# A linear-attention and MLP kernel: inverting the chunk triangles through the lower half's rows in 128 partitions, with one joining product instead of two

## The chip, the cores and the metric

The kernel runs on one core of one Trainium2 chip. The metric is the device time of the program in microseconds; three runs of the kernel before gave 593.81, 594.18 and 589.45 us, a median of 593.81. The profile is that of one further execution, of 596.33 us.

## The reference

A state matrix of 40 x 40 for each of 4 batches and 8 heads (32 in all) goes through 768 steps; its rows are read out before each step. What comes out is normalised and goes through an MLP with a residual.

```python
def _attn_ref(r, k, v, w, a, b):
    state = np.zeros((B, H, D, D))
    for t in range(S):
        y[:, :, t] = einsum('bhd,bhde->bhe', rt, state)
        Sa = einsum('bhde,bhe->bhd', state, at)
        state = state * wt[:, :, None, :] - einsum('bhd,bhe->bhde', Sa, bt) \
                + einsum('bhd,bhe->bhde', vt, kt)

def _moe_ref(x, g_ln, w_ch1, w_ch2):
    xn = (x - mean) / sqrt(var + 1e-06) * g_ln      # x: [4, 768, 320]
    return x + maximum(xn @ w_ch1, 0) @ w_ch2       # 320 -> 1280 -> 320
```

All inputs are float32: B, H, S, D = 4, 8, 768, 40.

## The kernel before

The 768 steps are cut into 24 chunks of C = 32 steps. Inside a chunk the dependence of a step on the earlier ones is a strictly lower triangular 32 x 32 matrix for each of the 32 heads (batch and head together), and the kernel needs the inverse of one plus that triangle. So a chunk has these parts:

- `prep` (L324): two scans on DVE (L338, L342) make running products of the decays; POOL multiplies them into the inputs (L350, L356; for chunks 0 and 1 DVE does it); PE forms all products of a chunk's steps with each other (L366); DVE gives them their sign and moves them out of PSUM (L369). One half of the result goes to DRAM as the triangles, `d_l`.
- `invert` (L396) makes the inverses. It works on a slab: chunks 0 and 1 are slabs of one chunk, done on DVE; all later slabs are two chunks, done on POOL. A triangle is one partition, so a slab of two chunks has 64 partitions of 32 x 32 elements.
- `merge` (L427) loads the inverted halves into `hv` in the layout that PE wants, and PE completes the inverse, `tt`.
- `chain` (L487): PE reads out the state with the chunk's rows (L498), ACT copies it (L501), PE multiplies by `tt` (L508), ACT copies that (L512), PE forms the state's update (L523) and DVE adds it (L532, L533). This is what one chunk must have of the one before.
- `post` (L540) makes the chunk's output rows from these (L551, L563, L578, L595).
- `norm` and `moe` normalise each chunk's 128 rows and run the MLP for two chunks at a time, in ten pairs of groups of dense matmuls: eight of L766 and six of L750 each. ACT (L769) and DVE (L771) stand between them.

The inverse in the kernel before is made of 16 x 16 halves (B = 16). A triangle [[P, 0], [Q, R]] has the inverse [[P', 0], [-R'QP', R']], with a prime for an inverse (the sign is in the data). `invert` inverts P and R at the same time, side by side in the free dimension of the same partition: for j from 1 to 14 a multiplication (L416) of column j by row j into `ytmp` and an addition (L420) into the rows below, over [64, 2, 15-j, j] elements. Before them stands a memset of the diagonal (L408), after them a copy on ACT that transposes R' (L422). A DMA stores P' and R' in `d_h`, and another copies Q from `d_l` to `d_h` inside DRAM (L425). `merge` then has two products: L441 forms QP' (16 columns) with an identity carried in the same operand, ACT copies it into `qm` (L443), and L452 forms the rest (32 columns), which ACT copies into `tt` (L454). Both have 32 matmuls, 8 heads in each of 4 quadrants of the array. The trace has two records for each.

What sets the order: `Plan` (L50) is given each operation with its engine, its assumed time in us, its due time (a key in chunks) and what it reads and writes. It goes through them as a list scheduler on an assumed clock and writes out one fixed order for each engine; the engines then work in that order and wait for each other by semaphores. An operation that is late on one engine so holds back all that stands behind the waiting one. Operations with `lock=True` on DVE and POOL are kept apart in the plan. DMAs are all issued from SP, in order, and take turns on eight semaphores, so that a DMA also waits for the one that was eight before it. In the plan a pair of L416 and L420 costs 0.54 us on DVE and 0.9 on POOL.

Of the kernel before, what the change touches and what calls it, by code (L numbers as in the profile page):

```python
# [11 lines left out]
F32 = mybir.dt.float32  # L12
# [4 lines left out]
ALU = mybir.AluOpType  # L17
# [4 lines left out]
C = 32  # L22
B = C // 2
# [159 lines left out]
def body(ctx, tc, ea, eb, vr, rd, vt, w1, w1x_in, w2, gl, fe, fd, out):  # L183
# [64 lines left out]
    d_h = [dr.tile([32 * n, B, 3 * B], F32, name=f"d_h{s}") for s, (_, n) in enumerate(SLABS)]  # L248
# [15 lines left out]
    def consts():  # L264
# [16 lines left out]
        for i in range(2):  # L281

            op("DVE", 0.9, -99 + i, (), [("wa", i, 0)], lambda i=i: V.memset(wa[i][32:64], 1.0))
        for i in range(BK):
            op("POOL", 0.9, -99 + i, (), [("bk", i, 0)], lambda i=i: G.memset(bk[i][32:64], 1.0))
        op("POOL", 0.3, -84, (), ["qm"], lambda: G.memset(qm, 0.0))
# [11 lines left out]
        for i in range(2):  # L298
# [3 lines left out]
            def f(i=i):  # L302
                for q, qs in enumerate(QUADS):
                    up, lo = (ident[qs, 32 * q + B * x:32 * q + B * x + B].unsqueeze(1).broadcast_to([32, 8, B])
                              for x in range(2))
                    A.copy(out=hv[i][qs, :, 0:B], in_=lo)
                    A.copy(out=hv[i][qs, :, 4 * B:5 * B], in_=up)
                    if i == 0:
                        A.copy(out=qm[qs, :, 0:B], in_=lo)
            op("ACT", 2.6 if i == 0 else 1.8, -50 + i, ["ident"], two("hv", i, 4) + (["qm"] if i == 0 else []), f)  # L310
# [85 lines left out]
    def invert(s):  # L396

        c0, n = SLABS[s]
        p0 = 32 * (c0 % 2)
        L = [("d_l", s, x) for x in range(2 * n)]  # L400
        Y = [("y", c0 % 2)] if n == 1 else [("y", 0), ("y", 1)]
        n *= 32
        eng, e, us = ("DVE", nc.vector, 0.54) if c0 < 2 else ("POOL", nc.gpsimd, 0.9)
        k0 = c0 - 2.0 - 2 * soon(c0)
        y = yv[p0:p0 + n]
        rows = y[:, 0:1024].rearrange("p (a t) -> p a t", t=C)
        dma(k0, 262, L, Y, y[:, 0:1024], d_l[s].rearrange("m a t -> m (a t)"))
        op(eng, 0.15, k0, (), Y, lambda: e.memset(y[:, 0:1024:33], 1.0))  # L408
        yb = y.rearrange("p (i x) -> p i x", i=2)[:, :, 0:512].rearrange("p i (a t) -> p i a t", t=C)[:, :, :, 0:B]
        for j in range(1, B - 1):  # L410
            m = B - 1 - j
            S = [n, 2, m, j]

            def f(j=j, m=m, S=S):
                tv = tmp[p0:p0 + n, 0:2 * m * j].rearrange("p (i a t) -> p i a t", i=2, t=j)
                e.tensor_tensor(  # L416
                    out=tv, in0=yb[:, :, j + 1:, j:j + 1].broadcast_to(S),
# [551 lines left out]
```

## Time and profile before

| what | value |
|---|---|
| runs, median (lowest to highest) | 593.81 us (589.45 to 594.18) |
| the profiled execution, its time | 596.33 us |
| its span in the profile | 594.6 us |
| mean granted clock of TensorE | 0.961 |
| PE busy | 517.6 us, 87% |
| DVE busy | 410.9 us, 69% |
| ACT busy | 311.2 us, 52% |
| POOL busy | 276.2 us, 46% |
| bytes moved by DMA | 58.58 MB in 119670 packets |

In the profile PE is the matmul stream of TensorE and PEld its loading of weights, which runs beside it; DVE is VectorE, ACT ScalarE, POOL GpSimd; SPq is the queue that issues the DMAs. A row of a list of groups has the line, the engine, the operation, the tiles written and read, the shapes and the count, then the busy time and the mean ns of one, then how long the engine stood idle just before them and what ended that. A row of the timeline has the start and the duration in us. In the view of the stretches the columns are the length, the busy time of PE, PEld, DVE, ACT and POOL with their counts, the granted clock, the busy share of the DMA engines and GB/s.

### The profile page before, as it was taken

The page shows a single profiled execution, that of the slowest core. Times are in us where ns is not written, and L with a number is a line of the kernel's source. Part 1 is how long each engine was busy: PE and PEld are TensorE (multiplying, and loading weights), DVE is VectorE, ACT ScalarE, POOL GpSimd, SP SyncE. Part 2 cuts the span into 40 slices and gives each one's busy share as a digit, 9 for nine tenths or more (in the row PEclk, how much of TensorE's full clock was granted, in tenths as well). Part 3 has the DMA queues.
Part 4 walks back from the last instruction along what each step waited for, and adds up shares of the span by engine and source line. Part 5 has one row for each costly group of instructions (what it writes and reads, how often), then busy time and mean ns, then how long its engine had stood idle before and what let it go on. Part 6 is the DMA issues. An engine that isn't in the chain of part 4 may idle for free.

```text
span 594.6 us, 33557 instructions
## 1 busy us (share of the span) xinstructions
PE 517.6 (87%) x14902; PEld 469.0 (79%) x14902; DVE 410.9 (69%) x907; ACT 311.2 (52%) x790; POOL 276.2 (46%) x510
## 2 busy tenths in 40 slices
PE   2527988799989899999899899899799899799996
PEld 2426766788879799888898798789799798688995
DVE  6699787787766667766676577686587667578622
ACT  8535768475465274373555365546456544555321
POOL 9425273374665572854824644674736706200000
PEclk9999779899989799998999899999999999899999
DMA  5465554425532435334243334434343344432000
GB/s 155 113 175 154 164 163 131 112 66 127 114 81 76 105 72 112 89 96 109 70 99 95 87 76 100 106 78 117 63 100 107 83 106 104 105 98 80 3 23 26
DMA packets 119670, 58.58 MB, mean 99 GB/s; under 512 B 100576, under 2 KB 106720, under 8 KB 119520
## 3 DMA queue, kind: packets, MB, share of 16 engines
q1 hardware_dynamic: 119520, 56.39, 38.6%
q8 instruction: 118, 1.93, 1.3%
q14 instruction: 32, 0.26, 0.1%
HBM read 44.56 MB, written 9.44 MB: 91 GB/s over the span
## 4 chain that ended last, share of the span: by engine, by line
PE 66%; POOL 8%; DVE 7%; issue 7%; ACT 5%; DMA 5%; SPq 1%; POOLq 0%; ACTq 0%; DVEq 0%
PE bank L750 17%; PE bank L766 16%; PE bank L366 4%; PE bank L578 4%; POOL ytmp L416 4%; POOL yv L420 4%; PE bank L595 2%; PE bank L498 2%; PE bank L508 2%; PE bank L441 2%; PE bank L452 2%; PE bank L563 2%; PE bank L473 2%; PE bank L523 2%; PE bank L551 2%
## 5 line engine op out<-in xcount | busy, mean ns | idle before, releaser
L750 PE MATMUL bank<-w,hh 128*128 128x320 f32 x480 | 119.9, 335 | 0.6 <-issue 0.6
L766 PE MATMUL bank<-xh,w 128*128 128x256 f32 x480 | 109.7, 290 | 4.4 <-issue 2.5
L769 ACT ACTIVATE hh<-bank 128x256 fp32r<-128x256 f32 x120 | 45.9, 384 | 116.4 <-PE bank L766 115.3
L771 DVE SCALAR_TENSOR_TENSOR hl<-bank,hh 128x256 fp32r<-128x256 f32 x120 | 49.9, 421 | 70.0 <-ACT hh L769 68.6
L766 PEld LDWEIGHTS bank<-xh,w 128*128 128x128 f32 x480 | 84.3, 193 | 4.4 <-issue 2.6
L750 PEld LDWEIGHTS bank<-w,hh 128*128 128x128 f32 x480 | 79.4, 195 | 7.6 <-issue 3.8
L356 POOL TENSOR_TENSOR bk<-bk,gE 104x1024 f32<-104x1024 f32 x22 | 48.9, 2222 | 65.7 <-issue 26.6
L750 PE MATMUL bank<-w,hl 128*128 128x320 f32 x240 | 76.2, 317 | 1.6 <-issue 1.6
L766 PE MATMUL bank<-xl,w 128*128 128x256 f32 x240 | 68.7, 286 | 0.2 <-issue 0.2
L350 POOL TENSOR_TENSOR x2s<-wa,qE 40x512 f32<-40x512 f32 x44 | 54.7, 1244 | 20.3 <-DVE qE L342 17.8
L420 POOL TENSOR_TENSOR yv<-yv,ytmp 64x28 f32<-64x28 f32 (+6 forms) x154 | 54.5, 354 | 12.1
L416 POOL TENSOR_TENSOR ytmp<-yv 64x28 f32<-64x28 f32 (+6 forms) x154 | 54.5, 354 | 11.4
L483 POOL MEMSET x5s<- 64x512 f32 x48 | 25.1, 522 | 71.6 <-PE bank L595 69.7
L532 DVE TENSOR_TENSOR bank<-bank,x 40x320 f32<-40x320 f32 x88 | 44.0, 500 | 11.2 <-PE bank L523 5.7
L478 ACT COPY xk<-bank 64x320 f32<-64x320 f32 x96 | 40.2, 419 | 21.7 <-PE bank L473 19.8
L584 DVE TENSOR_TENSOR x5s<-bank,mask 64x256 f32<-64x256 f32 x96 | 40.5, 422 | 15.4 <-PE bank L578 11.6
L766 PEld LDWEIGHTS bank<-xl,w 128*128 128x128 f32 x240 | 46.5, 194 | 3.1 <-issue 1.7
L750 PEld LDWEIGHTS bank<-w,hl 128*128 128x128 f32 x240 | 46.8, 195 | 1.4 <-issue 1.4
L512 ACT COPY x<-bank 32x320 f32<-32x320 f32 x96 | 40.1, 417 | 14.1 <-PE bank L508 12.8
L533 DVE TENSOR_TENSOR x<-bank,x2s 40x320 f32<-40x320 f32 x92 | 44.9, 489 | 3.1
L566 ACT COPY xk<-bank 40x320 f32<-40x320 f32 x96 | 40.2, 418 | 4.7 <-PE bank L563 3.0
L338 DVE TENSOR_TENSOR_SCAN gE<-wa,start 104x528 f32<-104x528 f32 x24 | 31.3, 1305 | 8.5 <-DMA wa<-in_ea_dram 4.8
(130 smaller groups left out, 1071.2 us busy)
## 6 DMA issues: line engine op xcount, KB each, us to landing
wa<-in_ea_dram SPq DMA_DIRECT2D x48, 162.7 KB
bk<-in_eb_dram SPq DMA_DIRECT2D x48, 160.0 KB
wa<-in_ea_dram SPq DMA_DIRECT2D x24, 165.0 KB
x<-in_vt_dram SPq DMA_DIRECT2D x48, 80.0 KB
x5s<-in_rd_dram SPq DMA_DIRECT2D x48, 80.0 KB
vu<-in_vr_dram SPq DMA_DIRECT2D x48, 80.0 KB
out_dram<-ot SPq DMA_DIRECT2D x24, 160.0 KB
r<-in_w_dram SPq DMA_DIRECT2D x10, 320.0 KB
```

The source lines that it names most:

```text
L350: op(eng, 0.75 * us, kp, W + [("q", i)], [("x2a", x, hf)], lambda hf=hf, rs=rs: e.tensor_tensor(out=x2s[x][rs, hf, 0:512].rearrange("p (h ...
L356: op(eng, 1.25 * us, kp, [("g", i)], K, lambda: e.tensor_tensor(out=kb, in0=kb, in1=g[R, :, 0:C].unsqueeze(2).broadcast_to([104, 16, 2, C] ...
L416: e.tensor_tensor(out=tv, in0=yb[:, :, j + 1:, j:j + 1].broadcast_to(S), in1=yb[:, :, j:j + 1, 0:j].broadcast_to(S), op=ALU.mult)
L420: e.tensor_tensor(out=v, in0=v, in1=tv, op=ALU.add)
L478: op("ACT", 0.45, c - 1.2 + 0.1 * bb, [bs[hf]], [X[hf]], lambda b=bs[hf], zs=zs, hf=hf, bb=bb: nc.scalar.copy(out=xk[i][zs, hf, 8 * bb:8 * ...
L532: nc.vector.tensor_tensor(out=p, in0=p, in1=x2[i][rs, hf, ps], op=ALU.add)
L533: nc.vector.tensor_tensor(out=x2[o][rs, hf, ps], in0=p, in1=x2s[xo][rs, hf, 512 + 8 * bb:520 + 8 * bb].unsqueeze(2).broadcast_to([D, 8, D] ...
L584: op("DVE", 0.46, k + 0.5, [b, "mask"], [("z", i)], lambda b=b, zs=zs, ps=ps, hf=hf, bb=bb: nc.vector.tensor_tensor(out=x5s[i][zs, hf, 8 * ...
L750: mm(bank_of(po[u])[:, 0:CH], lhsT=l[:, us], rhs=ws[f"w2_{f // 2}"][:, f % 2, x], start=f == 0 and n == 0, stop=f == 9 and n == 2)
L766: mm(ph, lhsT=l, rhs=r, start=n == 0, stop=n == 7)
L769: yield "ACT", 0.39, [phs[f]], [("hh", f % 2)], lambda f=f: nc.scalar.activation(out=hht[f % 2], in_=bank_of(phs[f])[:, 0:256], func=AF.Re ...
L771: yield "DVE", 0.46, [phs[f], ("hh", f % 2)], [("hl", f % 2)], lambda f=f: nc.vector.scalar_tensor_tensor(out=hlt[f % 2], in0=bank_of(phs[ ...
```

## The change

The inversion stays at the elimination of P, but goes on through the lower half's rows. If column j of P is eliminated in all rows below j, the lower left quarter ends as QP', and no product is needed for it. R' is got in the same instructions: each triangle now has two partitions. The left one (`yl`) holds the whole 32 x 32 triangle; the right one (`yr`) holds R moved to the upper left corner (the DMA loads it from element 33 x 16 on), with zeros or leftovers below. So a slab of two chunks has 128 partitions, and `[2n, 31-j, j]` elements for j from 1 to 15. ACT's copy transposes R' inside `yr`. Two stores, of 16 columns each, bring QP' with P' and the transposed R' to `d_h`. `hv` now carries an identity block at either end, and one product (L445 of the changed kernel) gives `tt`; `qm`, L441, L443 and the copy inside DRAM are gone.

```diff
-    tmp, = ring(1, "ytmp", 2 * 56)
-    hv = ring(2, "hv", 8, 5 * B)
-    qm, = ring(1, "qm", 8, C)
+    tmp, = ring(1, "ytmp", B * B)
+    hv = ring(2, "hv", 8, 4 * B)
...
     def invert(s):
...
-        dma(k0, 262, L, Y, y[:, 0:1024], d_l[s].rearrange("m a t -> m (a t)"))
-        op(eng, 0.15, k0, (), Y, lambda: e.memset(y[:, 0:1024:33], 1.0))
-        for j in range(1, B - 1):
-            m = B - 1 - j
-            S = [n, 2, m, j]
+        y, yl, yr = (yv[p0 + a * n:p0 + b * n] for a, b in ((0, 2), (0, 1), (1, 2)))
+        tri = d_l[s].rearrange("m a t -> m (a t)")
+        dma(k0, 131 * n // 32, L, [(*q, 0) for q in Y], yl[:, 0:1024], tri)
+        dma(k0, 64 * n // 32, L, [(*q, 1) for q in Y], yr[:, 0:1024 - 33 * B], tri[:, 33 * B:1024])
+        def f():
+            e.memset(y[:, 0:33 * B:33], 1.0)
+            e.memset(rows(yr)[:, 0:B, B:C], 0.0)
+        op(eng, 0.35, k0, (), Y, f)
+        yb = rows(y)[:, :, 0:B]
+        for j in range(1, B):
+            m = C - 1 - j
+            S = [2 * n, m, j]
             def f(j=j, m=m, S=S):
...
-            op(eng, us, k0 + 0.02 * j, (), Y, f, lock=True)
-        op("ACT", 0.68, k0 + 0.4, (), Y, lambda: nc.scalar.copy(
-            out=rows[:, 0:B, B:C], in_=rows[:, B:C, B:C].rearrange("p a k -> p k a")))
-        dma(k0 + 0.4, 131, Y, [("d_h", s, 0)], d_h[s][:, :, B:3 * B], rows[:, 0:B])
-        dma(k0 + 0.2, 280, L, [("d_h", s, 1)], d_h[s][:, :, 0:B], d_l[s][:, B:C, 0:B], 1024)
+            op(eng, 0.23 + 0.0021 * m * j if dve else 0.4 + 0.0036 * m * j, k0 + 0.02 * j, (), Y, f, lock=True)
+        op("ACT", 0.5, k0 + 0.4, (), Y, lambda: nc.scalar.copy(
+            out=rows(yr)[:, B:C, B:C], in_=rows(yr)[:, 0:B, 0:B].rearrange("p a k -> p k a")))
+        dma(k0 + 0.4, 100 * n // 32, Y, [("d_h", s, 1)], d_h[s][:, :, B:C], rows(yl)[:, :, 0:B], 1024)
+        dma(k0 + 0.4, 100 * n // 32, Y, [("d_h", s, 0)], d_h[s][:, :, 0:B], rows(yr)[:, :, B:C], 1024)
...
     def merge(c):
...
-                    mm(po[qs, h], lhsT=hv[i][qs, h, 0:2 * B], rhs=hv[i][qs, h, 3 * B:4 * B], start=True, stop=True)
-        op("PE", 0.66, km, two("hv", i, 4), [b], f, opens=[b], room=["qm"], recs=64.5)
-        op("ACT", 0.29, km, [b], ["qm"], ...)
-                    mm(po[qs, h], lhsT=qm[qs, h], rhs=right[qs, h], start=True, stop=True)
-        op("PE", 0.7, km, two("hv", i, 4) + ["qm"], [b], f, opens=[b], room=[("tt", i)], recs=64)
+                    mm(po[qs, h], lhsT=hv[i][qs, h, 0:C], rhs=hv[i][qs, h, C:2 * C], start=True, stop=True)
+        op("PE", 0.7, km, two("hv", i, 4), [b], f, opens=[b], room=[("tt", i)], recs=64.5)
```

The changed costs and operations also give another fixed order. Behind the functions that changed, a line of the changed kernel is 7 lower than the same line before (L759 is the old L766, L743 the old L750).

On SP, where the slab of chunks 18 and 19 goes through `invert` (`d_l_163` holds its triangles in both, `d_h_176` before and `d_h_175` now what was stored), the order was:

```order
L260 DMA yv_88<-d_l_163 64x1024
L260 DMA d_h_176<-d_l_163 1024x1x16
L260 DMA wa_76<-in_ea_dram 40x1041
L260 DMA bk_80<-in_eb_dram 40x1024 x2
L260 DMA wa_76<-in_ea_dram 40x1041
L260 DMA x_0_95<-in_vt_dram 32x640 x2
L780 DMA out_dram<-ot_142 128x320 x2
L260 DMA vu_105<-in_vr_dram 40x16x32 x2
L260 DMA d_h_176<-yv_88 1024x1x32
L260 DMA hv_90<-d_h_176 16x8x48 x4
```

and now, from the last loads ahead of the store on:

```order
L260 DMA x5s_100<-in_rd_dram 40x512 x2
L260 DMA x_1_95<-in_vt_dram 32x640
L260 DMA d_h_175<-yv_88 2048x1x16 x2
L260 DMA x_1_95<-in_vt_dram 32x640
L260 DMA wa_77<-in_ea_dram 40x1041 x2
L260 DMA hv_90<-d_h_175 32x8x32 x4
L260 DMA hv_91<-d_h_175 32x8x32 x4
```

One store of 1024 pieces of 32 elements has become two of 2048 pieces of 16, three loads have come between them and the load of `hv`, and the loads for both chunks now follow each other.

On ACT, around the copy that ends that slab's inversion (`yv_88<-yv_88`, L422 before), there stood:

```order
L566 COPY xk_103<-bank_148 40x320
L443 COPY qm_92<-bank_147 128x8x16
L353 COPY x2s_98<-gE_82 40x16
L422 COPY yv_88<-yv_88 64x16x16
L454 COPY tt_94<-bank_145 128x256
L501 ACTIVATE hn_108<-bank_148 128x320
L769 ACTIVATE hh_138<-bank_150 128x256
```

and now (L426 is the same copy, L762 the old L769, L547 the old L554):

```order
L559 COPY xk_103<-bank_145 40x320
L762 ACTIVATE hh_137<-bank_148 128x256
L426 COPY yv_88<-yv_88 64x16x16
L390 COPY pi_108<-bank_147 128x320
L387 COPY qc_87<-qE_84 104x512
L762 ACTIVATE hh_138<-bank_149 128x256
L547 COPY vu_105<-bank_145 40x16x32
```

The copy no longer stands between the two products of the chunk before it and its `tt`; what waits behind it now is the next chunk's preparation and an activation of the MLP.

On PE, at the first product of that slab (`hv_90`), there stood behind a row of transposes:

```order
L441 MATMUL bank_146<-hv_90 32x16 x32
L733 MATMUL bank_150<-ident,xn_118 128x128 x3
L750 MATMUL bank_151<-w_1_1433,hh_138 128x320 x2
L750 MATMUL bank_151<-w_1_1433,hl_140 128x320
L750 MATMUL bank_152<-w_1_1433,hh_138 128x320 x2
```

and now:

```order
L571 MATMUL bank_146<-x5s_101,vu_105 64x2x32 x16
L364 MATMUL bank_145<-x2s_97,bk_78 64x2x32 x16
L491 MATMUL bank_147<-x_0_94,x2s_98 32x40 x32
L743 MATMUL bank_150<-w_2_1495,hh_137 128x320 x2
L743 MATMUL bank_150<-w_2_1495,hl_139 128x320
L743 MATMUL bank_151<-w_2_1495,hh_137 128x320 x2
L743 MATMUL bank_151<-w_2_1495,hl_139 128x320
L759 MATMUL bank_148<-xh_134,w_3_1535 128x256
```

with the rest of that group and then `L445 MATMUL bank_144<-hv_90 32x32 x32`. The product has moved from ahead of the read-out of its chunk (L498, now L491) to behind it, and between it and the preparation of chunk 19 (L366 before) there are now 22 groups of dense matmuls (a group is eight of L766 or six of L750), where there were 16.

More of the change, by code (lines that the diff above doesn't have):

```diff
@@ L305, in f @@
                               for x in range(2))
[L306 to L310, printed above, removed]
+                    A.copy(out=hv[i][qs, :, 0:B], in_=up)
+                    A.copy(out=hv[i][qs, :, 3 * B:4 * B], in_=lo)
+            op("ACT", 1.8, -50 + i, ["ident"], two("hv", i, 4), f)
             op("POOL", 1.0, -40 + i, (), [("uT", i)] + two("vT", i), lambda i=i: G.memset(vu[i], 0.0))
```

38 lines of the change are left out of this document (14 added, 24 removed).

## The prediction

> **What bounds the kernel now.** I read the page's busy shares first, then its chain that ended last, then the busy times by stretch.
>
> ```profile
> span 594.6 us, 33557 instructions
> PE 517.6 (87%) x14902; PEld 469.0 (79%) x14902; DVE 410.9 (69%) x907; ACT 311.2 (52%) x790; POOL 276.2 (46%) x510
> PE 66%; POOL 8%; DVE 7%; issue 7%; ACT 5%; DMA 5%; SPq 1%; POOLq 0%; ACTq 0%; DVEq 0%
> PE bank L750 17%; PE bank L766 16%; PE bank L366 4%; PE bank L578 4%; POOL ytmp L416 4%; POOL yv L420 4%; PE bank L595 2%; PE bank L498 2%; PE bank L508 2%; PE bank L441 2%; PE bank L452 2%; PE bank L563 2%; PE bank L473 2%; PE bank L523 2%; PE bank L551 2%
> ```
>
> ```profile
> 0.00:60.00 60.00, 26.98 (x928) 23.62 (x930) 47.88 (x116) 33.37 (x83) 32.40 (x53) 1.00 0.57 149
> 60.00:100.00 40.00, 34.94 (x708) 27.33 (x706) 32.83 (x64) 29.57 (x72) 20.58 (x39) 0.79 0.53 147
> 100.00:131.00 31.00, 26.71 (x755) 23.58 (x753) 22.88 (x48) 18.67 (x44) 15.53 (x36) 0.94 0.44 107
> 131.00:523.20 392.20, 364.87 (x11299) 333.58 (x11295) 268.66 (x589) 205.49 (x531) 206.64 (x381) 0.97 0.40 95
> 523.20:594.60 71.40, 64.14 (x1239) 60.92 (x1237) 38.70 (x94) 24.12 (x63) 1.04 (x2) 0.98 0.15 45
> ```
>
> The columns are the stretch, its length, and the busy time of PE, PEld, DVE, ACT and POOL. From 131 us on (chunk 4 to chunk 22) PE is busy 364.9 of 392.2 us, 93%; POOL 53%, DVE 69%. So in the long stretch PE's own work sets the pace, and what others do counts only where PE's fixed order waits for it. Until 60 us PE is busy 27 us: there a chain through DVE, DMA and POOL sets the pace. The 8% of POOL on the chain is the other thing to see: nearly all of it is the inversion (L416 and L420, 4% each), so that is not everywhere hidden. The change makes PE's work smaller and exactly that inversion longer. The question is which of the two wins.
>
> **The term that is removed: one product a chunk.**
>
> ```profile
> L441 PE MATMUL bank<-hv 32*32 32x16 f32 x1344 | 16.1, 181 | 3.7 <-issue 3.5
> L443 ACT COPY qm<-bank 128x128 f32<-128x128 f32 x21 | 5.6, 266 | 7.8 <-PE bank L441 7.7
> PE bank L441 <- issue: 3.5, 2, 2.7
> ```
>
> From 100 to 560 us L441 takes 16.1 us for 21 chunks (64 matmul records each), 0.767 us a chunk. The product that stays is one of the old L452's shape, so nothing is added for it. Chunks 0 and 1 stand in the starting chain and are counted there; for the other 22 I take 22 x 0.767 = **-16.9 us**. Bounds: 0 (all of it becomes waiting) and -16.9. L443's 24 x 0.266 = 6.4 us of ACT go too, counted at nothing: ACT is busy 52% and the copy was 0.27 us. PE also stands idle with no releaser: the rows named "issue" in PE's waits, of which the largest is shown, add to 21.9 us. 1536 of PE's 14902 records go, 10.3%, so **-2 us** (bounds 0, and -5.6, all that L441 and L452 have in that view, 3.5 and 2.1).
>
> **The term that grows: the inversion on POOL.** An inversion was 28 instructions of 28 to 112 elements; it becomes 30 of (31-j)j elements, 30 to 240, and a second memset. The elements go from 2 x 1120 = 2240 to 2 x 2480 = 4960. Twice as many partitions I take as free: nothing in the trace separates them.
>
> ```profile
> 72.34 0.17 POOL L408 MEMSET yv<- 64x32 f32 x1
> 72.42 0.25 POOL L416 TENSOR_TENSOR ytmp<-yv 64x28 f32<-64x28 f32 x1
> 72.75 0.25 POOL L420 TENSOR_TENSOR yv<-yv,ytmp 64x28 f32<-64x28 f32 x1
> ...
> 77.30 0.40 POOL L416 TENSOR_TENSOR ytmp<-yv 64x112 f32<-64x112 f32 x1
> 77.77 0.40 POOL L420 TENSOR_TENSOR yv<-yv,ytmp 64x112 f32<-64x112 f32 x1
> ...
> 83.70 0.24 POOL L420 TENSOR_TENSOR yv<-yv,ytmp 64x28 f32<-64x28 f32 x1
> ...
> 494.75 0.15 POOL L408 MEMSET yv<- 64x32 f32 x1 [11.94 <-DMA yv<-d_l]
> 507.81 0.23 POOL L420 TENSOR_TENSOR yv<-yv,ytmp 64x28 f32<-64x28 f32 x1
> ```
>
> Start to start is 0.33 us at 28 elements and 0.47 at 112, so 0.28 us an instruction and 1.7 ns an element. That gives 30 x 0.28 + 4960 x 1.7 ns = 17.0 us, 17.3 with the memsets, against 11.6 in this slab (72.34 to 83.94; slabs are named by their first chunk, this is slab 2). The eleven slabs took 11.6 to 13.3 (the last rows), mean 12.2, 5% over the quiet one; so 18.2 against 12.2, **+6.0 us a slab** on POOL. In the code the planner now prices a pair at 0.4 + 0.0036mj, in all 14.9 us, where it had 12.6. So it holds room for 2.3 more, and POOL will be about 3 us late by its plan.
>
> The way from POOL to the product goes on through ACT's copy, the store, and the load of hv.
>
> ```profile
> 126.98 0.24 POOL L420 TENSOR_TENSOR yv<-yv,ytmp 64x28 f32<-64x28 f32 x1
> 128.28 0.66 ACT L422 COPY yv<-yv 64x256 f32<-64x256 f32 x1
> ...
> 132.53 2.05 SPq L260 DMA_DIRECT2D hv<-d_h  x4
> 136.40 0.73 PE L441 MATMUL bank<-hv 32*32 32x16 f32 x64
> ...
> 422.11 0.61 SPq L260 DMA_DIRECT2D d_h<-yv  x1
> 424.80 2.65 SPq L260 DMA_DIRECT2D hv<-d_h  x4
> ...
> 511.45 4.65 SPq L260 DMA_DIRECT2D hv<-d_h  x8
> 520.69 0.73 PE L441 MATMUL bank<-hv 32*32 32x16 f32 x64
> ```
>
> One store of 1024 packets (0.61 us to issue) becomes two of 2048 packets of 64 bytes; the copy from DRAM to DRAM goes and a second load comes, which even out on SP. The second store adds 0.6 us of issue. Landing: the old store had landed 2.08 us after its issue (422.72 to 424.80). Bounds are 0, and 4 times the packets at all of it, +6.2. The loads of hv, of 128 packets each, need up to 1.8 us too (134.58 to 136.40), so some 0.3 us of the 2.08 is transfer; four times that is **+1.0**, which I take. In all the way is 6.0 + 0.6 + 1.0 = 7.6 us longer.
>
> The Trainium skill (DMA: Bandwidth & Descriptors, "Why small descriptors are slow") adds a fixed three cycles or so to a packet's 32-byte beats, which makes 4096 packets of 64 bytes 2.9 times the work of 1024 of 128. Were the 2.08 us all transfer, that would be +3.9 where I take +1.0, and the sum would go to the slow rival below.
>
> **What of it is given back.** Counted through the new order of PE, what stands between the second chunk's L366 and the slab's first product grows, mean of ten slabs, from 16.7 to 18.9 groups of dense matmuls, and some small products.
>
> ```profile
> 427.20 1.08 PE bank L750 x6
> 428.28 0.96 PE bank L766 x8
> ```
>
> 2.2 groups are 2.2 us at these rows, and the small products some 1.8 us: **4.0 us**. Another 1.0 is hidden because ACT comes late: POOL had ended at 127.22 and the copy began at 128.28, and so in six of eleven slabs (mean 1.8 us). So a slab's hv comes 7.6 - 4.0 - 1.0 = 2.6 us later against PE than now. How much slack is there? From the end of issue of the first four loads to L441 were 1.8 us in slab 4 (so landing takes at most that) and some 6.9 in slab 22; less 1.8, the ten slabs have 0, 6.1, 0.2, 4.9, 5.2, 2.7, 1.2, 0.7, 3.5 and 5.1 us. With 2.6 us the stalls are 2.6 + 2.4 + 1.4 + 1.9, **+8.3 us** (bounds 0, and 26 at 5.5 us late, as in the slow rival). The next to be late behind POOL is this:
>
> ```profile
> ACT yv L422 <- POOL yv L420: 11.4, 4, 4.9
> 423.57 1.15 PE L366 MATMUL bank<-x2s,bk 104*64 104x64 f32 x32 [0.69 <-POOL bk L356]
> 426.01 0.48 PE L473 MATMUL bank<-ident,bk 40*64 40x40 f32 x16 [1.28 <-DVE xt L599]
> ```
>
> ACT's copy waited 11.4 us in four slabs, everything behind it on ACT waited too, and PE lost the 0.69 and 1.28 us shown. These are the same lateness and are not added again.
>
> **The start.** Chunks 0 and 1 are inverted on DVE.
>
> ```profile
> L420 DVE TENSOR_TENSOR yv<-yv,ytmp 32x112 f32<-32x112 f32 x4 | 1.1, 263 | 0.1
> L420 DVE TENSOR_TENSOR yv<-yv,ytmp 32x28 f32<-32x28 f32 x4 | 0.7, 186 | 0.1
> 30.76 0.09 DVE L408 MEMSET yv<- 32x32 f32 x1
> 38.34 1.26 DVE L338 TENSOR_TENSOR_SCAN gE<-wa,start 104x528 f32<-104x528 f32 x1
> 38.49 1.46 PE L441 MATMUL bank<-hv 32*32 32x16 f32 x64 [12.23 <-DMA hv<-d_h]
> ```
>
> 0.92 ns an element and 0.16 us, with the gap of 0.03 that makes 28 instructions last the 7.6 us from 30.76 to 38.34, give 30 x 0.19 + 4.6 + 0.2 = 10.5 us, 3.2 more a slab. Chunk 2's scan (38.34) starts right behind, so 6.4 us later, and slab 2's inversion is longer as well: +12.4 at worst. Against it: the first product falls out of a wait (2 us, L441 to L452), two conversions of w1x (3.1 us) move ahead of the inversion, and PE's order puts 72 dense matmuls before chunk 3's L498 instead of 30, 5 us that are done early. I take **+3 us** (bounds 0 and +12.4).
>
> **Sum:** -16.9 - 2 + 3 + 8.3 = **-7.6 us** on the span of 594.6, whose execution took 596.33. The three runs have a median of 593.81, 2.5 us below that execution; so 593.8 - 7.6 = **586.2 us**, -1.3%. Its own range is 582 to 591.
>
> **Rivals.**
>
> *All hidden.* The 2.6 us meet a reordered plan with more slack; stalls 0, start +2: -17, **577 us**. For it: PE waited for hv once in all, in the start. Against it: three slabs have under 0.8 us of slack.
>
> *Gain eaten.* Late by 4 us instead of 2.6 (ACT's lateness gives nothing back): stalls 4 + 3.8 + 1.3 + 2.8 + 3.3 + 0.5 = 15.7, sum -0.2, **593.6 us**.
>
> *The inversion sets the slab's pace (slower).* Late by 5.5 us: stalls 26, start +5, sum +12, **606 us**. One mechanism: POOL's instruction waits while DVE scans.
>
> ```profile
> 163.96 1.24 DVE L338 TENSOR_TENSOR_SCAN gE<-wa,start 104x528 f32<-104x528 f32 x1
> 164.06 1.29 POOL L416 TENSOR_TENSOR ytmp<-yv 64x88 f32<-64x88 f32 x1
> ```
>
> An instruction of 88 elements, about 0.36 us by the rows at 28 and 112, took 1.29 us here: 0.9 us a scan. A slab has four such scans (L338 and L342 of two chunks). If all four fall into the inversion, that is 3.6 us and not the 0.9 that I count, 2.7 more: 5.3 us late. For it: the inversion becomes half as long again, and the plan, which keeps the two apart, is 3 us too short for it. Against it: mean cost now 0.6. It decides from about 4.8 us late on; there the sum passes +6 us, 1%. The Trainium skill (SBUF — State Buffer, "Who interferes with whom") calls the port that the two share an exclusive lock held for a whole instruction; this row agrees, and by that rule alone all four scans could cost this.
>
> *The product's time is not PE's to save.* If each 0.767 us only becomes waiting for another engine, 0 + 3 + 8.3 gives **605 us**. Against it: PE's 93% in the long stretch.
>
> **How the numbers follow.** The forecast 0.36, all hidden 0.16, gain eaten 0.24, slow inversion 0.21, no saving 0.03. Below 574 us there is no mechanism but more relief from "issue"; 607 us holds the slow rivals' middle; so the range is 574 to 607. About 1% (6 us) is what a measurement of this kernel can tell from no change. Faster by more than that: all of the hidden case, six tenths of the forecast (whose middle is 1.6 us beyond the line) and a little of the eaten one, 0.41. Within 1%: the rest of the forecast and over half of the eaten case, 0.31. Slower: the slow cases and what of the eaten one lies above, 0.28.
>
> **What would show it.** Right, step by step: in the groups, L441 and L443 are gone and L445 takes 0.75 to 0.8 us a chunk; a POOL inversion lasts 17.3 us quiet and about 18.2 in the mean, and POOL's busy time goes from 276 to about 330 us; chunk 2's scan on DVE starts near 45 us; ACT's copy L426 waits for POOL in more than four slabs; PE waits for hv by 1 to 3 us in some four slabs beside the first one. PE's busy time falls to some 501 us. The tail behind chunk 23 stays as it is, since the order of PE puts 432 dense matmuls behind the last L498 and had 426.
>
> Wrong would be: inversions below 16 us (then the time is near 577), waits on hv or on ACT behind L426 in nearly every slab (then 600 and more), or a PE that is as long idle "issue" as before with no wait on hv, so that the loss is in the reordered plan and not in the inversion.

## The result and the profile after

The change makes the kernel slower: **617.49 us** (median of 4 runs, 614.26 to 621.04) against 591.63 (4 runs of the kernel before on the same chip), a ratio of 1.044 with a 95% interval of 1.0351 to 1.0530. The forecast was 586.2 and the range ended at 607. The profiled execution after took 621.04 us, with a span of 619.2. A ratio here is of the executions outside a slower state that some executions of a kernel fall into, so it need not be the quotient of the two medians.

The page after: span, busy time by engine, and the first lines of the chain that ended last.

```profile
span 619.2 us, 30534 instructions
PE 513.3 (83%) x13366; PEld 463.9 (75%) x13366; DVE 426.0 (69%) x913; ACT 307.4 (50%) x762; POOL 346.0 (56%) x543
PE 37%; POOL 28%; DMA 6%; issue 5%; ACT 3%; SPq 2%; DVE 1%; POOLq 0%; ACTq 0%
```

1536 matmul records are gone as meant, but PE's busy time fell by 4.3 us only (517.6 to 513.3), and PE's idle time grew from 77.0 us (594.6 - 517.6) to 105.9. That is the whole difference of the spans: 28.9 - 4.3 = 24.6 us. POOL's share of the chain went from 8% to 28%.

The busy times by stretch, in the columns of the prediction's table. The bounds are the first products on the chain (L491, before L498) of chunks 4 and 22.

```profile
0.00:60.00 60.00, 22.61 (x575) 19.57 (x577) 48.90 (x109) 31.49 (x74) 28.12 (x47) 1.00 0.57 145
60.00:144.80 84.80, 69.16 (x1633) 57.92 (x1630) 66.25 (x132) 52.01 (x123) 58.91 (x89) 0.88 0.53 125
144.80:548.30 403.50, 358.00 (x9994) 326.39 (x9994) 270.62 (x579) 199.99 (x504) 257.95 (x406) 0.92 0.43 96
548.30:619.20 70.90, 63.51 (x1174) 59.99 (x1173) 40.26 (x96) 23.94 (x62) 1.04 (x2) 0.98 0.17 50
```

Chunk 4 comes at 144.8 us and not at 131, **13.7 us** lost in the start. From chunk 4 to chunk 22 it takes 403.5 us and not 392.2, **11.3 us** more, though there is less to do. The tail is the same (70.9 and 71.4). Two things stand in the long stretch's row: PE is idle for 45.5 us instead of 27.3, and its granted clock is 0.92 instead of 0.97. What the clock withheld is 8% of 403.5 = 32 us, where it was 3% of 392.2 = 12 us.

The inversion itself, slab 6 on the changed kernel's timeline:

```profile
162.12 0.13 POOL L411 MEMSET yv<- 128x16 f32 x1 [5.02 <-DMA yv<-d_l]
...
178.78 0.63 ACT L426 COPY yv<-yv 64x256 f32<-64x256 f32 x1 [2.62 <-POOL yv L424]
179.53 0.65 POOL L424 TENSOR_TENSOR yv<-yv,ytmp 128x240 f32<-128x240 f32 x1
180.20 1.65 SPq L260 DMA_DIRECT2D d_h<-yv  x2
...
185.07 1.80 SPq L260 DMA_DIRECT2D hv<-d_h  x4
```

From 162.12 to 180.18 are 18.1 us. The eleven slabs took 18.0 to 20.6, mean 18.9, against 11.6 to 13.3 and 12.1 before. ACT's copy needs nothing of the last pair of steps, so it begins before POOL ends; the store waits for POOL. The planner holds 14.9 us for the pairs and 0.35 for the memsets, so its order is written for an inversion that ends 2.8 us earlier than the quiet one and 3.6 us earlier than the mean.

The waits for POOL and for hv, after (time in all, times, longest):

```profile
ACT yv L426 <- POOL yv L424: 37.0, 11, 5.9
PE bank L364 <- POOL bk L354: 10.3, 6, 4.3
PE bank L364 <- POOL x2s L348: 4.9, 2, 2.8
PE bank L445 <- DMA hv<-d_h: 16.5, 1, 16.5
```

ACT's copy waits for POOL in all eleven slabs, 37.0 us (before 11.4 in four). PE waits for hv once, in the start, as before. So hv is not what comes late for PE. What does is shown by slab 16 first:

```profile
398.78 0.62 ACT L426 COPY yv<-yv 64x256 f32<-64x256 f32 x1 [4.21 <-POOL yv L424]
399.43 0.20 ACT L710 ACTIVATE sd<-ve 128x1 f32<-128x1 f32 x1
399.52 0.64 POOL L424 TENSOR_TENSOR yv<-yv,ytmp 128x240 f32<-128x240 f32 x1
399.66 0.16 DVE L713 RECIPROCAL r<-sd 128x1 f32<-128x1 f32 x1 [5.80 <-ACT sd L710]
400.12 2.19 POOL L354 TENSOR_TENSOR bk<-bk,gE 104x1024 f32<-104x1024 f32 x1
402.36 1.97 PE L364 MATMUL bank<-x2s,bk 104*64 104x64 f32 x32 [4.33 <-POOL bk L354]
```

Two engines stand in the inversion's shadow. ACT stood 4.2 us at the copy, with the norm's root (L710) behind it, and DVE waited 5.8 us for that. POOL itself came to bk (L354), the next chunk's operand, only behind the inversion, and PE, whose fixed order had the product of x2s and bk (L364) next, stood 4.33 us. The same place by stretches:

```profile
398.00:402.30 4.30, 0.04 (x1) 0.00 (x0) 2.50 (x5) 1.67 (x4) 4.06 (x5) 0.86 0.15 19
402.30:407.80 5.50, 5.44 (x47) 5.32 (x48) 4.72 (x10) 1.01 (x3) 5.13 (x8) 0.50 0.53 82
407.80:414.00 6.20, 6.20 (x182) 5.65 (x181) 4.62 (x9) 4.08 (x11) 1.52 (x1) 0.99 0.33 62
```

Around the end of the wait the granted clock goes to 0.50, and stays there for 5.5 us. PE is busy all the time, but its matmuls take longer: L364's 32 took 1.97 us here and 1.20 us at 147.50 (last section). If all work of that stretch took up to twice as long, the wait of 4.3 us cost up to 7 us; that is an estimate.

The longest wait of the stretch came by way of ACT, in slab 14:

```profile
355.17 0.63 ACT L426 COPY yv<-yv 64x256 f32<-64x256 f32 x1 [5.88 <-POOL yv L424]
356.58 0.24 ACT L721 COPY xn<-xn 128x64 f32<-128x64 f32 x1
356.88 0.48 PE L726 MATMUL bank<-ident,xn 128*128 128x128 f32 x1 [4.59 <-ACT xn L721]
```

DVE had written xn by 350.80 us (L718), but ACT's copy of its last columns (L721) stood behind L426, and PE stood 4.59 us for it. Of the eight waits of PE of 1.86 us and more between chunks 4 and 22, five (15.1 us) end with work that stood on ACT behind L426, one of these by way of DVE, and three (8.3 us) with POOL's bk or x2s, which POOL reached without a pause behind an inversion.

### The profile page after: what moved, and what is told of

The parts are those of the page before. It is cut to its first block, busy times and chain, and to the rows that moved or that the text cites. A ratio compares the mean times of both kernels' runs of the same rounds, so it can differ in the third digit from the quotient of the medians.

```text
span 619.2 us, 30534 instructions
## 1 busy us (share of the span) xinstructions
PE 513.3 (83%) x13366; PEld 463.9 (75%) x13366; DVE 426.0 (69%) x913; ACT 307.4 (50%) x762; POOL 346.0 (56%) x543
## 4 chain that ended last, share of the span: by engine, by line
PE 37%; POOL 28%; DMA 6%; issue 5%; ACT 3%; SPq 2%; DVE 1%; POOLq 0%; ACTq 0%
PE bank L743 12%; POOL yv L424 11%; POOL ytmp L421 11%; PE bank L759 10%; DMA yv<-d_l 3%; PE bank L364 3%; POOL bk L354 2%; PE bank L571 2%; PE bank L556 2%; SPq L260 2%; PE bank L445 2%; POOL x2s L348 2%; DMA x5s<-in_rd_dram 1%; PE bank L588 1%; ACT x L505 1%
## 5 line engine op out<-in xcount | busy, mean ns | idle before, releaser
L743 PE MATMUL bank<-w,hh 128*128 128x320 f32 x480 | 123.1, 343 | 0.1
L759 PE MATMUL bank<-xh,w 128*128 128x256 f32 x480 | 111.7, 295 | 3.6 <-DVE hl L764 2.0
L762 ACT ACTIVATE hh<-bank 128x256 fp32r<-128x256 f32 x120 | 46.0, 384 | 114.4 <-PE bank L759 113.5
L424 POOL TENSOR_TENSOR yv<-yv,ytmp 128x30 f32<-128x30 f32 (+4 forms) x165 | 90.1, 546 | 12.9
L421 POOL TENSOR_TENSOR ytmp<-yv 128x30 f32<-128x30 f32 (+4 forms) x165 | 86.2, 522 | 13.0
L759 PEld LDWEIGHTS bank<-xh,w 128*128 128x128 f32 x480 | 86.8, 199 | 5.7 <-DVE hl L764 2.2
L743 PEld LDWEIGHTS bank<-w,hh 128*128 128x128 f32 x480 | 81.8, 201 | 5.3 <-issue 0.9
L743 PE MATMUL bank<-w,hl 128*128 128x320 f32 x240 | 77.4, 323 | 0.9 <-issue 0.8
L354 POOL TENSOR_TENSOR bk<-bk,gE 104x1024 f32<-104x1024 f32 x22 | 48.5, 2205 | 48.7 <-DVE gE L336 24.4
L759 PE MATMUL bank<-xl,w 128*128 128x256 f32 x240 | 69.8, 291 | 0.8 <-issue 0.8
L364 PE MATMUL bank<-x2s,bk 104*64 104x64 f32 x768 | 32.9, 250 | 31.1 <-DVE bk L354 12.1
L364 PEld LDWEIGHTS bank<-x2s,bk 104*64 104x64 f32 x768 | 29.6, 162 | 33.4 <-POOL x5s L316 12.1
L525 DVE TENSOR_TENSOR bank<-bank,x 40x320 f32<-40x320 f32 x88 | 44.0, 500 | 12.5 <-PE bank L516 10.2
L471 ACT COPY xk<-bank 64x320 f32<-64x320 f32 x96 | 40.1, 418 | 20.0 <-PE bank L466 18.2
L759 PEld LDWEIGHTS bank<-xl,w 128*128 128x128 f32 x240 | 47.8, 199 | 1.2 <-issue 1.0
L743 PEld LDWEIGHTS bank<-w,hl 128*128 128x128 f32 x240 | 48.4, 202 | 0.0
L559 ACT COPY xk<-bank 40x320 f32<-40x320 f32 x96 | 40.0, 417 | 13.6 <-PE bank L556 11.9
```

The lines of the kernel that those rows point to most:

```text
L354: op(eng, 1.25 * us, kp, [("g", i)], K, lambda: e.tensor_tensor(out=kb, in0=kb, in1=g[R, :, 0:C].unsqueeze(2).broadcast_to([104, 16, 2, C] ...
L364: mm(pg[64 * bb:64 * bb + 64, :, h], lhsT=tb[R, 64 * p:64 * p + 64], rhs=x2s[x][R, :, 32 * p:32 * p + 32], start=True, stop=True)
L421: e.tensor_tensor(out=tv, in0=yb[:, j + 1:, j:j + 1].broadcast_to(S), in1=yb[:, j:j + 1, 0:j].broadcast_to(S), op=ALU.mult)
L424: e.tensor_tensor(out=v, in0=v, in1=tv, op=ALU.add)
L525: nc.vector.tensor_tensor(out=p, in0=p, in1=x2[i][rs, hf, ps], op=ALU.add)
L743: mm(bank_of(po[u])[:, 0:CH], lhsT=l[:, us], rhs=ws[f"w2_{f // 2}"][:, f % 2, x], start=f == 0 and n == 0, stop=f == 9 and n == 2)
```

## The experiments

Theories ahead of the runs: **order** (the fixed order is written for an inversion that is too short, and the engines that it stops cost the time); **length** (18 us on POOL and 11 on DVE cost it whatever the order); **stores** (pieces of 64 bytes, two stores). All ratios are to the kernel before on the same chip; its median there moved between 593.4 and 597.1 us from one set of runs to the next, so ratios count and not the times alone.

**1. The prices right (e1_true_prices).**

```
-op(eng, 0.23 + 0.0021 * m * j if dve else 0.4 + 0.0036 * m * j, ...
+op(eng, 0.36 + 0.0019 * m * j if dve else 0.58 + 0.0034 * m * j, ...
-op("ACT", 0.5, k0 + 0.4, (), Y, ...
+op("ACT", 0.65, k0 + 0.4, (), Y, ...
```

> The changed kernel with the planner's prices put right by the rows: 0.58 + 0.0034mj us for a pair of steps on POOL (17.4 us an inversion where the plan held 14.9), 0.36 + 0.0019mj on DVE, 0.65 for ACT's copy. The instructions are the same, only their order changes. Theory 'order' (an order written for inversions 2 to 3 us too short holds up ACT and POOL in every slab): the wait of ACT's copy for POOL falls from 37 us to under 15, and at least half of the loss of 25 us goes, 595 to 605 us. Theory 'length' (an inversion of 17 us on POOL and of 10 us on DVE costs the time whatever the order): 612 to 620 us. Theory 'stores' (more and smaller pieces to DRAM): 612 to 620 us as well.

Measured: **595.89 us**, ratio 1.0023 (0.9975 to 1.0072). Only the order of the instructions is different, and of the 4.4% of loss 0.2% is left. The inversions last as long as in the changed kernel (mean 18.7 us).

```profile
ACT yv L426 <- POOL yv L424: 13.9, 8, 2.9
PE bank L364 <- POOL bk L354: 6.6, 3, 3.2
145.30:524.50 379.20, 347.85 (x9925) 317.35 (x9922) 269.72 (x573) 199.61 (x503) 263.24 (x407) 0.95 0.45 100
```

The long stretch takes 379.2 us: 24.3 less than the changed kernel's, and 13.0 less than before's, which is most of the product's 16.9. The start's loss stays (chunk 4 at 145.3). Against the changed kernel's stretch PE is idle 14.1 us less (31.4 and 45.5) and busy 10.2 us less (347.8 and 358.0), with nearly the same matmuls in it (9925 and 9994 records). Order holds; length and stores, as reasons for the 11.3 us of the stretch, fall.

**2. and 3. A short inversion, with the prices right (e2_short_pool, e3_short_both).** Both leave out the inversion's last four steps, so they do not compute the whole inverse.

```
 e2:
-for j in range(1, B):
+for j in range(1, B if dve else 12):
 e3:
-for j in range(1, B):
+for j in range(1, 12):
```

> As with the prices put right, and POOL's inversion leaves out its last four steps (j of 12 to 15), so that it lasts about 12 us as in the kernel before; the two inversions on DVE keep all steps, and stores and loads stay. Part of the computation is left out. Theory 'length': the loss between chunks 4 and 22 (11.5 us) goes and the saved product shows there, the start's 13.7 us stay in part: 590 to 600 us. Theory 'order': little is left to gain beyond the prices, within 5 us of the run with the prices alone. Theory 'stores': over 605 us.

> As the one before, and the two inversions on DVE leave out the same four steps too, so that they last 7.1 us instead of 10.3. Theory 'length': the start's loss goes as well, and the time is the kernel's before less the product: 575 to 583 us. Theory 'order': within 5 us of the run with the prices alone. Theory 'stores': over 600 us.

Measured: e2 **593.20 us**, ratio 0.9996 (0.9952 to 1.0039); e3 **581.89 us**, 0.9792 (0.9719 to 0.9865). Making POOL's inversion 5.8 us a slab shorter (mean 12.9) gains 0.3% on e1, within the intervals: at the right price its length is hidden. Shortening the two on DVE as well gains 2%, and chunk 4 comes at 138.4 us instead of 144.9: that is 6.5 of the 8.0 us between the two spans. So what the length costs by these two runs, it costs in the start. In e2 ACT's copy still waits for POOL in all eleven slabs, 30.7 us in all, but PE waits only 0.3 us for bk: how long the copy waits does not by itself say what it costs.

**4. and 11. A third store, on the change's prices and on the right ones (e4_third_store, e11_third_store_priced).**

```
+dma(k0 + 0.4, 100 * n // 32, Y, [("d_x", s)], d_x[s][:, :, 0:B], rows(yr)[:, :, B:C], 1024)
 dma(k0 + 0.4, 100 * n // 32, Y, [("d_h", s, 1)], d_h[s][:, :, B:C], rows(yl)[:, :, 0:B], 1024)
```

> The changed kernel with one store more a slab: the right half's columns go a second time, to a place in DRAM that nothing reads, ahead of the two stores that hv needs. That makes 3 stores of 64-byte pieces where there were 2. Theory 'stores': a slab's hv comes some 2.5 us later again and the time grows by 5 us or more, to over 622 us. Theories 'order' and 'length': hv has slack and PE does not wait for it, so within 4 us of the changed kernel, 613 to 621 us.

> The run with the three prices right and the third store of 64-byte pieces a slab, which reads the right half's columns and which nothing needs. On the change's own prices that store cost 9.7 us. Theory 'stores' (the store as such delays hv, or holds SP): 8 us or more over the run with the prices, 603 to 610 us. Theory 'order' (the store only made an order worse that was late anyway): within 4 us, 592 to 600 us.

Measured: e4 **627.23 us**, ratio 1.0573 (1.0482 to 1.0665), so 9.7 us over the changed kernel, as "stores" had it; e11 **599.87 us**, 1.0146 (1.0043 to 1.0249), 4 us over e1, at the edge of what "order" allowed. By the medians a store of 64-byte pieces is not free, and it costs more where the order is late already; the intervals are too wide for a factor. In e4 PE's longest waits in the stretch (7.0 and 6.2 us) are for work on ACT, whose copy waits 43.8 us in nine slabs, and PE waits only 1.0 us for bk. The store cannot be the changed kernel's loss, since e1 has the same two stores and not the loss.

**5. and 6. POOL's price alone, right and too high (e5_pool_price, e6_over_price).**

```
 e5:
-0.4 + 0.0036 * m * j
+0.58 + 0.0034 * m * j
 e6:
-0.4 + 0.0036 * m * j
+0.76 + 0.0036 * m * j
```

> The changed kernel with one price put right alone, that of a pair of steps on POOL (0.58 + 0.0034mj us); DVE's and ACT's stay as in the change. Theory 'order, by POOL's price': all of the gain of the run with the three prices comes with it, 592 to 600 us. Theory 'order, by DVE's price at the start': the gain stays away, over 610 us. Theory 'luck' (any new order moves the time by as much): somewhere between 590 and 625.

> As the last, but POOL's pair at 0.76 + 0.0036mj us, 20.7 us with the memsets where the inversion lasts 18.0 undisturbed: as far above it as the change's 15.3 is below. Theory 'order': what costs is an inversion that ends later than planned, not one that ends earlier, so near the run with the right price, 592 to 603 us. Theory 'luck': no better than the changed kernel, 605 to 625 us.

Measured: e5 **594.02 us**, ratio 0.9955 (0.9910 to 1.0000); e6 **597.67 us**, 1.0005 (0.9963 to 1.0046). POOL's price does it alone. An inversion planned 2.8 us too short costs 4.4%, one planned 2.7 us too long costs no more than e1's order. This also speaks against luck: three orders with a long enough inversion land within 0.7% of each other. (Not every order with the right price does: see e10.) e5 is the best here of the kernels that compute everything, but its interval ends at 1.0000, so it is not shown to beat the kernel before.

The page of e5:

```profile
PE 501.5 (84%) x13366; PEld 452.3 (76%) x13366; DVE 420.9 (71%) x913; ACT 305.6 (51%) x762; POOL 349.5 (59%) x543
```

PE's busy time is 16.1 us under before's 517.6, at a mean granted clock of 0.958 (before 0.961). The prediction's 16.9 us of saved product are there. In the changed kernel, at 0.931, they were not to be seen.

**7. The kernel before, with its price too low (e7_before_under).**

```
-("POOL", nc.gpsimd, 0.9)
+("POOL", nc.gpsimd, 0.63)
```

> The kernel before, with two products and its inversion of 11.6 us undisturbed, but the planner's price of a pair on POOL 0.63 us instead of 0.9: the plan holds 9.0 us with the memset, 2.6 us too few, as many as the change's prices are short. The instructions are the same. Theory 'order': it loses as the change did in the long stretch, slower than before by 8 to 25 us, 600 to 620. Theory 'length' (it is the 18 us themselves that cannot be hidden when they are planned short): within 5 us of before, 590 to 600 us.

Measured: **619.61 us**, ratio 1.0395 (1.0244 to 1.0546). With two products and the short inversion, none of the change in it, the kernel loses about what the changed one loses: 14.7 us up to chunk 4 (145.8 and 131.1), 9.3 us from chunk 4 to chunk 22 (401.4 and 392.1), and the tail gives 4.2 back. The row of the copy's wait in this kernel could be taken for the changed one's:

```profile
ACT yv L422 <- POOL yv L420: 36.2, 11, 5.9
```

This is the strongest run against "length". It does not say by which engine the loss comes to PE: here PE's waits for POOL are small (3.5 us in three), and the waits that grew are mostly for ACT (xk 3.0 to 7.2 us, qm 0.5 to 5.9). It also shows that a late chunk 4 needs no long inversion on DVE.

**8. and 10. The start: one joint inversion, or one of two on POOL (e8_joint_start, e10_chunk1_pool).** Both with the prices of e1.

```
 e8:
-SLABS = [(0, 1), (1, 1)] + [(c, 2) for c in range(2, NCH, 2)]
+SLABS = [(c, 2) for c in range(0, NCH, 2)]
 e10:
-dve = c0 < 2
+dve = c0 < 1
```

> The changed kernel with the three prices right, and chunks 0 and 1 as one slab: one inversion on DVE in 128 partitions instead of two in 64. By the rows of the run with the right prices it begins when chunk 1's triangles are there (about 29 us) and ends about 40 us, where the two ended at about 46. Theory 'the start's loss is the two long inversions on DVE': chunk 4's first product on the chain (now 145.3 us) comes 4 to 8 us earlier and the time falls to 586 to 592 us. Theory 'the start's loss is POOL's longer inversion behind it': no more than 2 us, 593 to 597 us.

> The three prices right, and chunk 1 inverted on POOL instead of DVE: DVE has one inversion in the start, and chunk 2's scan can begin near 36 us instead of 47, while POOL, idle there, takes 18 us for chunk 1 from about 29 us on. Theory 'the start's loss is DVE's second long inversion': chunk 4's first product on the chain comes 5 to 10 us earlier than 145.3 and the time falls to 585 to 591 us. Theory 'something else in the start is the bound': 593 to 599 us.

Measured: e8 **598.23 us**, ratio 0.9986 (0.9921 to 1.0051); e10 **610.46 us**, 1.0295 (1.0206 to 1.0383). In e8 chunk 4 does come 4.7 us earlier (140.6), but chunk 1 now waits for both (70.1 instead of 55.4) and the long stretch takes 385.4 us instead of 379.2. In e10 chunk 1's first product on the chain comes at 69.9, chunk 4's at 145.2, and the stretch takes 389.5. In e8 chunk 4 came as early as was expected of a start bound by the long inversions on DVE, but the time did not fall; e10 missed both of its ranges. Less DVE time in the start did not shorten the whole; in e10, though, POOL takes 18 us for what takes DVE 11. e10 also shows that the right price alone does not keep the inversions on time: ACT's copy waits for POOL in ten slabs there (26.3 us), and PE for bk in six (10.0 us).

**9. and 12. Which of the two late engines (e9_late_copy, e12_late_next).** On the change's own prices. The empty tasks exist for the planner only.

```
 e9:
+if not dve:
+    op("X", 2.9, k0 + 0.4, (), Y, lambda: None)
 op("ACT", 0.5, k0 + 0.4, (), Y, ...
 e12:
-op(eng, 0.23 + ..., k0 + 0.02 * j, (), Y, f, lock=True)
+op(eng, 0.23 + ..., k0 + 0.02 * j, (), Y + [("gap", s)], f, lock=True)
+if not dve:
+    op("POOL", 2.9, k0 + 0.3, (), [("gap", s)], lambda: None, lock=True)
```

> The changed kernel with its prices as they are; only, the planner takes ACT's copy behind an inversion on POOL (and so the stores and hv) for possible 2.9 us later than POOL's last step, by an empty task on no engine. No instruction is added. POOL's own next work stays planned too early. Theory 'ACT' (what costs is that ACT, in order, stands at the copy for 2 to 6 us a slab, and with it everything behind it): the 37 us of that wait fall under 15, and most of the 22 us that the right price brought come here too, 595 to 604 us. Theory 'POOL' (what costs is POOL's next work, bk and x2s of the chunks that follow, late for PE's product): 608 to 618 us.

> The complement of the run with the late copy: the change's prices stay, ACT's copy is planned right behind POOL's last step as in the change, but an empty task of 2.9 us holds POOL in the plan behind each inversion, so that only POOL's own next work (bk and x2s of the chunks that follow, and with them PE's product of the two) is planned later. No instruction is added. Theory 'POOL' (the loss is PE standing at its product of x2s and bk, which POOL finishes late): that wait falls from 10 us and more under 5, ACT's wait for POOL stays above 25 us, and the time is that of the right price, 592 to 602 us. Theory 'both waits are needed' (either of the two late engines costs it all): 610 to 620 us.

Measured: e9 **620.10 us**, ratio 1.0478 (1.0374 to 1.0583); e12 **598.45 us**, 1.0097 (1.0061 to 1.0133). In e9:

```profile
ACT yv L428 <- POOL yv L424: 4.8, 4, 2.8
PE bank L364 <- POOL bk L354: 23.6, 8, 3.9
```

In e12:

```profile
ACT yv L428 <- POOL yv L424: 22.1, 9, 4.0
PE bank L364 <- POOL x2s L348: 1.7, 1, 1.7
```

Taking ACT's wait away gained nothing: the time came back as PE's wait for bk, which rose from 10.3 to 23.6 us. My first theory of the mechanism, ACT's copy, falls as the sole cause. Planning POOL's next work later removes PE's wait for bk, leaves 22.1 us of ACT's wait, and gains 3.4 of the 4.4%. ACT's wait was expected above 25 us and is a little under. What e12 lacks against e5 (1.0097 and 0.9955) may be what ACT's lateness still costs once POOL's is cured, but that was not tried by itself and is not shown: e2 has more of ACT's wait without the loss, PE also waits for hv eleven times in e12 beside the start (4.9 us), and other orders with the right price differ by as much. The empty task also keeps DVE's locked operations away in the plan, so e12 moves more than POOL's work.

**13. The start done the old way (e13_old_start).** POOL's price as in e5.

```
 def invert(s):
     c0, n = SLABS[s]
+    if c0 < 2:
+        return invert_old(s)
...
 def merge(c):
...
+    if c < 2:
...
+                mm(po[qs, h], lhsT=ho[i][qs, h, 0:2 * B], rhs=ho[i][qs, h, 3 * B:4 * B], start=True, stop=True)
...
+                mm(po[qs, h], lhsT=qm[qs, h], rhs=right[qs, h], start=True, stop=True)
...
```

> POOL's price right (0.58 + 0.0034mj us), and chunks 0 and 1 done as in the kernel before, with its short inversion on DVE (7.6 us instead of 11.2) and two products; chunks 2 to 23 as in the change. Theory 'the start's loss is DVE's two long inversions' (7 us on DVE): chunk 4's first product on the chain comes at 131 to 139 us instead of 144 to 145, the long stretch stays at 374 to 386 us, and the kernel beats both, 580 to 590 us. Theory 'the start is late by POOL's longer inversion of slab 2 and by the order there': 592 to 598 us.

Measured: **596.52 us**, ratio 1.0110 (1.0065 to 1.0156).

```profile
60.00:133.70 73.70, 60.31 (x1321) 49.85 (x1321) 56.37 (x113) 47.74 (x113) 43.85 (x73) 0.86 0.55 130
133.70:517.60 383.90, 359.94 (x10002) 327.83 (x9998) 275.98 (x580) 202.70 (x509) 264.04 (x411) 0.94 0.45 100
517.60:593.40 75.80, 64.13 (x1227) 60.18 (x1223) 42.65 (x101) 24.21 (x62) 4.78 (x8) 0.96 0.24 61
```

Chunk 4 comes at 133.7 us, 10.1 earlier than in e5 (143.8): with chunks 0 and 1 done the old way most of the start's loss is gone. That need not all be DVE's two inversions, since their products and stores change with them, and in e6, which keeps the long inversions, chunk 4 comes at 138.7. But the earlier start does not shorten the kernel. Against e5 the stretch takes 5.4 us more and the tail 2.5, so 7.9 of the 10.1 are given back in the profiled executions, and in the medians all of it. So no version here beats the kernel before beyond doubt and computes everything. Why an earlier start is given back in e8 and e13, and not in e3, stays open: the order is made anew each time, and the stretches of the kernels with POOL's price right that compute everything scatter from 378.5 us (e5) to 389.5 (e10).

## Why the prediction was wrong

**The step that failed is the stall term**, "So a slab's hv comes 7.6 - 4.0 - 1.0 = 2.6 us later against PE than now" with its "+8.3 us". It was to cost four waits of PE for hv. The lateness was sized well, but it was followed along one path only, POOL to hv to the product, and that path had the slack: PE waited for hv once in all, in the start. Two things were queued behind the longer inversion and were not followed. On POOL itself it is the next chunks' bk and x2s; on ACT, which stands in order at the copy, it is everything of the norm and the chain. By these two PE's waits of 1.86 us and more came to 23.3 us in the stretch, 8.3 and 15.1, with a lower clock behind them. The prediction named both ("The next to be late behind POOL is this"), quoted their rows, and dropped them as "the same lateness and are not added again". They are other consumers of the same lateness, with slacks of their own. It even wrote that the plan "holds room for 2.3 more, and POOL will be about 3 us late by its plan". By e1 and e5 putting that right takes the long stretch's loss away, and by e7 the same shortfall alone makes a loss of its kind.

**Point by point.** The product: 16.9 us predicted, 16.1 in e5's busy time; in the changed kernel 4.3 are seen and 12.6 are lost again, where its clock withheld 20 us more than before's (32 and 12). POOL's price: +6.0 a slab predicted, 12.1 to 18.9 = +6.8 measured; the quiet inversion is 18.0 and not 17.3. The stores' way: from the end of their issue to the loads of hv are 3.2 us (181.85 to 185.07) where it was 2.08, which is 1.1 us more where 1.0 was predicted; both are upper bounds of the landing. By the Trainium skill's fixed cost for a packet (DMA: Bandwidth & Descriptors, "Why small descriptors are slow") the prediction had worked out, as an estimate, 3.9 us more, were all of the 2.08 us transfer; the trace does not bear that out. POOL's busy time is 346.0, a little over the "about 330". PE's idle time with no releaser fell from 21.9 to 11.5 us, more than the 2 that was taken and than the bound of 5.6. Two sums are slightly off: 30 x 0.28 + 4960 x 1.7 ns is 16.8 us and not 17.0, and from 7.6 to 10.5 us are 2.9 and not 3.2; neither decides anything. Chunk 2's scan on DVE was predicted near 45 us:

```profile
35.12 0.07 DVE L411 MEMSET yv<- 64x16 f32 x1
...
46.05 0.41 DVE L424 TENSOR_TENSOR yv<-yv,ytmp 64x240 f32<-64x240 f32 x1
46.48 1.26 DVE L336 TENSOR_TENSOR_SCAN gE<-wa,start 104x528 f32<-104x528 f32 x1
```

It came at 46.48, since an inversion on DVE takes 11.3 us and not 10.5. **The start** was the second mis-sized term: "+3 us (bounds 0 and +12.4)" where 13.7 came, over the bound. Of the reliefs that were set against the 12.4 (an earlier product, conversions moved ahead, more dense matmuls before chunk 3) nothing is seen in it. What made it is open in part: e13's old way of doing chunks 0 and 1 takes 10.1 off, a higher price alone takes 5.1 off (e6 against e5), and e7 has a late chunk 4 without any of the change. The tail stayed, as predicted.

**The rivals.** "The inversion sets the slab's pace" had the right sign and named the short plan, but its mechanism, scans of DVE that block POOL's instructions, is not it: the interference stayed at 0.9 us a slab (mean 18.9, quiet 18.0), and e1 has the same inversions without the loss. Its point of decision, "about 4.8 us late", was computed on hv's slack; POOL's and ACT's own slack is smaller, and some 3 us were enough. "The product's time is not PE's to save" is refuted by e1's stretch. The text's own sign of being wrong, waits "on ACT behind L426 in nearly every slab (then 600 and more)", is what the trace shows, with L426 itself waiting in all eleven. By itself it is a weak sign, since e2 has that too, at 593.20 us.

**What a stall of PE costs** was missing from every case: each was counted at its own length, and the clock behind it was not counted at all. The Trainium skill (TensorE: Matmul & The Clock Gate, "The HAM clock gate") says that an idle window of about 3.4 us halves PE's clock, and that about as long of sustained work brings it back. The rows at 402.3 us agree with the half clock. By that rule a stall of 3 us would be free of it; here shorter stalls had the half clock behind them, as the last section shows.

## What to carry to other kernels

In a kernel whose order is fixed by a planner's prices, the price of a changed instruction is part of the change: measure it, start to start and with the gaps, and put it right before the change is judged; too high cost little here and too low cost 4%. When a step on an in-order engine grows, list everything that stands behind it on that engine and behind whoever waits for it, and take each one's slack; the path that the change is about may be the one with room. And where TensorE is 93% busy, price a stall of 2 us and more above its own length: against e1 and e5, which have the same 13366 matmul records, the changed kernel's PE is idle 19.4 and 11.8 us longer, and with that also busy 5.4 and 11.8 us longer.

## What the hardware showed

**Behind short stalls TensorE's clock was half.** At 147.5 us L364 had stood for 1.86 us behind POOL. Its row, and the stretches before and behind it:

```profile
147.50 1.20 PE L364 MATMUL bank<-x2s,bk 104*64 104x64 f32 x32 [1.86 <-POOL bk L354]
```

```profile
144.80:148.00 3.20, 1.34 (x80) 1.22 (x82) 2.06 (x5) 0.72 (x2) 3.06 (x3) 1.00 0.69 181
148.00:155.00 7.00, 7.00 (x226) 6.16 (x224) 4.82 (x8) 2.60 (x8) 1.86 (x5) 0.53 0.54 79
```

The clock was 0.53 over the 7 us that follow, in which PE was never idle: 3.3 us withheld for 1.86 us of waiting. Read in steps of 1 us from chunk 4 to chunk 22, the clock withheld 30.7 us in the changed kernel, 11.9 in the one before, 15.4 in e5 and 18.2 in e1. In the changed kernel all eight waits of 1.86 us and more there, 23.3 us, have such a drop, of 3.41 or 6.83 us at half clock, that begins between 1.3 us before their end and 2.3 us behind it: 23.9 us withheld. Three more drops came behind idle times of PE of 0.9 to 1.62 us, and in the kernel before one came at 172.59 us behind no idle time of 0.9 us. That the drops are set off by the waits is read from their place in time; no run made a wait and nothing else.

**A small tensor_tensor on GpSimd** took its time by its elements a partition, and twice as many partitions cost nothing that is seen. The group of the smallest form in the changed kernel:

```profile
L424 POOL TENSOR_TENSOR yv<-yv,ytmp 128x30 f32<-128x30 f32 x11 | 2.9, 265 | 0.9
```

30 elements in 128 partitions take 0.265 us in the mean, and the prediction's rows have 0.25 for 28 elements in 64. Likewise 108 elements in 128 partitions took 0.37 and 0.41 us (164.95 and 165.39 us), and the prediction's 112 in 64 took 0.40. The 240 elements at 399.52 take 0.64.
